# A gated long convolution and a SwiGLU FFN on one core: block order, a radix-4 transform for block 1, residuals by accumulating DMA, and a last tile in halves

## The chip, the cores and the metric

One Trainium2 chip, one core of it. The metric is device time in microseconds (us): the median of the runs of a kernel, smaller is better. Inputs and outputs are bf16; sums run in float32 in PSUM.

## The reference

For x = A_q (2048 tokens of 640 channels), with ln a layer norm without weights:

```python
k_shift = sum over t of pad(k)[t : t + S] * shift_k[:, 3 - t]      # 4 taps, causal
kv = k_shift * v
y  = irfft(rfft(kv, 2 S) * rfft(ssm_k, 2 S))[:S] + kv * ssm_D      # causal convolution of length 2048, per channel
h  = x + ln(x) * y
g, u = silu(ln(h) @ w_gate), ln(h) @ w_up                          # 640 -> 1728
out  = h + (g * u) @ w_down                                        # 1728 -> 640
```

## The kernel before

**Blocks.** The 2048 tokens are four blocks of 512. The convolution is done by blocks: each block's signal kv (`XH`) and each block of the filter (`C[0..3]`) are transformed once, and output block i is the inverse transform of a sum of products `prod(j, i)` over j <= i, kept in `Y[i]`. A task p12 is the product of signal block 1 that goes into output block 2. The filter's blocks are combined with their neighbours first (`kcomb`, L652).

**Transforms (L557 to L650).** A block of 512 tokens is read as 128 partitions by 4 token groups j (token 4p + j), so a transform is four matmul parts, one for each j, and butterflies on VectorE between them. Three forms stand side by side: `fulls` (L576) leaves all to TensorE, 64 matmuls of 128 x 320; `halves` (L557) takes 32 and one pair of additions; `quads` (L594) takes 16 and six additions in two stages. Block 0's signal goes by `fulls`, block 1's by `halves`, blocks 2 and 3 by `quads` (`R4X = (2,3)`, L354). The inverse has a two-part form (blocks 0 and 1) and a four-part form (`iquads`, blocks 2 and 3). In the two-part form token groups 0 and 2 read one of the sums (`OS`), groups 1 and 3 the other.

**Gate and second norm (`inverse`, L831).** For each token group j: matmuls (`iv`), an eviction on ScalarE that scales by the first norm's reciprocal deviation and adds 1 (`e`), a product with the centred x on VectorE (`g`: this is h less its mean), mean and squares on ScalarE (`m`, `s`), a small addition on VectorE (`v`), a power of -0.5 on GpSimd (`r`, L781), the normalization on VectorE (`n`, L912), and a transposing DMA from SP's queue into `hnT` (`ht`, L436).

**FFN (`ffn`, L917).** Each block's FFN runs in two halves of 256 tokens, that is token groups 0 and 1, then 2 and 3. Matmuls into `ps` (L943), silu and copy on ScalarE (L951, L956), the product on VectorE (L964). Then four down products `dn` (L1026), one for each token group, of 28 matmuls of 320 columns into two PSUM banks. `rs` (L1041) reads PSUM, adds the mean of x and the residual in `xh` on VectorE, and `out` stores 160 KB from SP's queue.

**Accumulating DMA.** `addto` (L553) issues from GpSimd's queue a DMA that adds one SBUF tile into another. The kernel uses it for seven half or whole products and for one sum of the filter's block 3.

**Order.** The work is a list of tasks (`_Graph.add`, L92) with their reads and writes. The order on each engine is written out by hand in `PLAN` (L256) as task numbers; a task waits for the tasks it depends on, and each engine works its list strictly in order. The lists also choose between ScalarE and VectorE where a task may run on both, and give each matmul group one of four PSUM units of two banks, which it shares in turn: a group's first matmul waits until the unit's former content has been read. `fills` puts dummy matmuls ahead of a named task: 7 ahead of `wb0` (L496) and 4 ahead of `kt0.1` (L533). SP's list holds loads, transposing DMAs and stores: a DMA whose data isn't ready holds up those behind it.

Of the kernel before, what the change touches and what calls it, by code (L numbers as in the profile page):

```python
# [50 lines left out]
class _Graph:  # L51
# [128 lines left out]
    def emit(self, block):  # L180
# [85 lines left out]
    "act":  # L266
# [10 lines left out]
    "dve":  # L277
# [10 lines left out]
    "pool":  # L288
        "17 15 16 121 159 122 168 216 186 177 226 335 336 355 364 389 394 373 382 404 399 507 532 541 559 566 550 571 674 699 "
        "708 726 717 "  # L290
        "",
    "sp":
        "0 4 2 3 6 7 10 8 236 13 9 11 293 12 14 229 228 230 294 231 461 227 292 161 232 170 188 179 235 234 462 233 628 357 366 "
        "291 282 288 285 460 375 384 629 453 534 543 456 450 459 627 561 552 701 620 710 719 728 617 777 623 626 780 774 783 "
        "",
    "units":
        "0101323321220010313213100231120202332120102331301320022011320202230231210230113011022111311232002332032013120133100202"
        "11223112023230123210032310310302310311023011302103021130213"
        "",
    "fills": {  # L300
        "wb0": ["zmem", 7],
        "kt0.1": ["zmem", 4],
# [4 lines left out]
def bass_sequential_preLN__ssm_conv_h3__swiglu_ffn__prompt_kernel(  # L307
# [34 lines left out]
    LO = (('k',3),)  # L342
# [7 lines left out]
    R4X = (2,3)  # L350
# [19 lines left out]
    with ExitStack() as es:  # L370
# [33 lines left out]
        nitab = sb("nitab", 150784 + 2048, [2, 2, 2, P])  # L404
# [9 lines left out]
        bns = sb("bns", 187936, [4, 2, 6], f32)  # L414
        mvs = sb("mvs", 187936 + 192, [4, 2], f32)
# [178 lines left out]
        def quads(name, src, dst, tmp, scale, rot):  # L594
            spot = {(0, 0): dst[:, 0, 0], (0, 1): dst[:, 0, 1], (2, 0): tmp[:, 0, 0], (2, 1): tmp[:, 0, 1],
                    (3, 1): dst[:, 1, 0], (1, 0): dst[:, 1, 1], (1, 1): tmp[:, 1, 0], (3, 0): tmp[:, 1, 1]}
            for j in (1, 3, 0, 2):
                for cs in range(2):
# [12 lines left out]
            flip = dst[:, 2]  # L611
            flip = bass.AP(flip.tensor, flip.offset + D, [list(flip.ap[0]), [-D, 2], [1, D]])
            tt2 = (("0", flip, dst[:, 1], tmp[:, 1], ALU.add, 2), ("1", dst[:, 3], dst[:, 1], tmp[:, 1], ALU.subtract, 2),
                   ("2", tmp[:, 1], dst[:, 0], tmp[:, 0], ALU.subtract, 2), ("3", tmp[:, 0], dst[:, 0], tmp[:, 0], ALU.add, 2),
                   ("4", dst[:, 0:2], tmp[:], dst[:, 2:4], ALU.add, 4), ("5", dst[:, 2:4], tmp[:], dst[:, 2:4], ALU.subtract, 4))
            for q, d, a, b, op, n in tt2:
                g.add("%s.%s" % (nm, q), "dve", lambda e, n_, d=d, a=a, b=b, op=op: e.tensor_tensor(out=d, in0=a, in1=b, op=op), ("sb", n * D),  # L617
                      r=[a, b], w=[d])

        def iquads(i):  # L620
            y = Y[i]

            def two(f0, c0, step):
# [5 lines left out]
                   ("4", y[:, 1:4:2], OS[:], y[:, 0:3:2], ALU.add, 4), ("5", y[:, 0:3:2], OS[:], y[:, 0:3:2], ALU.subtract, 4))  # L629
            for q, d, a, b, op, n in tt2:  # L630
                g.add("yb%d.%s" % (i, q), "dve", lambda e, n_, d=d, a=a, b=b, op=op: e.tensor_tensor(out=d, in0=a, in1=b, op=op), ("sb", n * D),
                      r=[a, b], w=[d])

# [18 lines left out]
        def kcomb(m, dst, own, prev):  # L652
            if m in KD:
                for f in range(2):
                    addto("kc%d.%d" % (m, f), dst[:, 2 * f:2 * f + 2], own[:, 2 * f:2 * f + 2])
                return
            g.add("kc%d.s" % m, "dve", lambda e, n: e.tensor_tensor(out=dst[:], in0=prev[:], in1=own[:], op=ALU.add), ("sb", 8 * D),  # L657
                  r=[own[:], prev[:]], w=[dst[:]])
# [61 lines left out]
        def prod(j, i):  # L720
# [43 lines left out]
            if i == j and i in R4Y:  # L764
                iquads(i)
            elif i == j and ("y", i) in MB:
# [46 lines left out]

        def hntile(i, j, q, hold):
            if i or i in HT0:
                tload("ht%d.%d" % (i, j), hnT[:, :, j * P:(j + 1) * P], q[:], P, D, r=[q[:]])
                return
            if j % 2 == 0:
                hold[0] = g.tile()
            pt, b = hold[0], j % 2  # L820
# [6 lines left out]
            g.add("hp%d.%d" % (i, j), "pe", tr, ("tr", 5), r=[q[:], ident], pw=[pt])  # L827
            d = hnT[:, :, j * P:(j + 1) * P]
            evac("hpe%d.%d" % (i, j), (d, d), lambda pt=pt, b=b: pt.h(b, 0, D).rearrange("p (c x) -> p c x", c=NC5), D, pt)

        def inverse(i):  # L831
            hold = [None]
            for j in range(4):
# [3 lines left out]
                src = Y[i][:] if full else Y[i][:, (1, 3, 0, 2)[j]] if i in R4Y else (OS[:], Y[i][:, 2:4])[j % 2]  # L837
# [21 lines left out]
                nm = "iv%d.%d" % (i, j)  # L859
# [55 lines left out]
                hntile(i, j, q, hold)  # L915

        def ffn(i):  # L917
# [89 lines left out]
            for j in range(4):  # L1007
# [5 lines left out]
                if j % 2:  # L1013
                    seq = [13] + seq[:-1]
                parts = [seq[:-4], seq[-4:]] if j == 0 else [seq]
                for part in parts:

                    def mm(e, n, pt=pt, j=j, part=part, seq=seq, x2=x2):
                        for fb in part:
                            for c in range(2):  # L1020
# [5 lines left out]
                                last = e.matmul(pt.f(c, W), gu[k, fb, j * P:(j + 1) * P], Wd[k, fb, c * W:(c + 1) * W], start=st, stop=sp)  # L1026
# [4 lines left out]
                    g.add("dn%d.%d%s" % (i, j, "b" if len(parts) > 1 and part is parts[1] else ""), "pe", mm,  # L1031
                          ("mm", W, 2 * len(part) - (13 in part)) + mode,
                          r=[gu[:, f, j * P:(j + 1) * P] for f in fbs] + [Wd[:, f] for f in fbs] + ([x, ident] if "id" in part else []),
                          pw=[pt])
                nm = "rs%d.%d" % (i, j)
# [13 lines left out]
                g.add("out%d.%d" % (i, j), "sp", lambda e, n, x=x, od=od: e.dma_start(od, x), ("st", 163840), r=[x], dma=True)  # L1049
# [17 lines left out]
        prod(0, 1)  # L1067
        ktrans(3)
        kfwd(3, K3r)
        kcomb(3, K2r, K3r, K2r)  # L1070
        prod(0, 3)
        prod(0, 2)
        gview = B_w_gate.rearrange("(c p) f -> p c f", p=P)
        uview = B_w_up.rearrange("(c p) f -> p c f", p=P)
# [57 lines left out]
```

## Time and profile before

| | us |
|---|---|
| median of 3 runs | 262.49 (261.42 to 262.93) |
| the profiled execution | 261.17 |
| its span, first to last instruction | 259.4 |
| TensorE matmul busy | 253.9 |
| VectorE busy | 204.9 |
| ScalarE busy | 185.8 |
| GpSimd busy | 44.6 |

In the profile's rows PE is TensorE's matmuls, PEld its weight loads, DVE VectorE, ACT ScalarE, POOL GpSimd, SP the queue that issues most DMAs. L1026 is line 1026 of the kernel before. A group's row reads: line, engine, operation, output <- inputs, sizes, count | busy us, mean ns of one | idle time of the engine just before them and what ended it. In the strips each digit is the busy share of one fortieth of the span in tenths. Matmuls overlap, so the length of one (about 0.3 us) is longer than its step to the next. The granted TensorE clock was 1.00 over the span.

### The profile page before, as it was taken

The numbers are of one execution on the slowest core, as the hardware profiler recorded it, in microseconds if no ns is written. First come the engines' busy times: TensorE is split into PE (matmuls) and PEld (weight loads), VectorE is DVE, ScalarE is ACT, GpSimd is POOL, SyncE is SP. The second block draws the span as 40 slices with busy tenths as digits, with TensorE's granted clock in tenths as the row PEclk, the third lists the DMA queues.
The fourth block names the chain that finished last, engine by engine and source line by source line (L and its number), as shares of the span: only waits on it lengthen the run. The fifth ranks groups of instructions, "written<-read, shape, count | busy, mean of one in ns | idle before, by whom it ended". The sixth has DMA issues, their size and how long they took to land.

```text
span 259.4 us, 5381 instructions
## 1 busy us (share of the span) xinstructions
PE 253.9 (98%) x2308; PEld 199.8 (77%) x2308; DVE 204.9 (79%) x249; ACT 185.8 (72%) x311; POOL 44.6 (17%) x37
## 2 busy tenths in 40 slices
PE   7999999999999999999999999999999999999995
PEld 2787786688888866778888766888886678888663
DVE  2899999999999999998999989999996732110323
ACT  2799999997965777977776979896976445653400
POOL 0000031625402013426030141041001101000000
PEclk9999999999999999999999999999999999999999
DMA  6999997170299500198638006389000110200022
GB/s 192 378 259 316 386 240 248 30 136 4 56 330 203 107 0 3 32 221 196 162 57 149 0 0 75 95 188 153 3 0 0 31 48 20 60 3 0 3 76 76
DMA packets 34117, 29.41 MB, mean 113 GB/s; under 512 B 20899, under 2 KB 30510, under 8 KB 34094
## 3 DMA queue, kind: packets, MB, share of 16 engines
q1 hardware_dynamic: 31648, 23.82, 33.4%
q0 software_dynamic: 2432, 5.24, 11.7%
q8 instruction: 18, 0.29, 0.5%
q14 instruction: 5, 0.04, 0.0%
q10 hardware_dynamic: 14, 0.01, 0.0%
HBM read 16.55 MB, written 2.62 MB: 74 GB/s over the span
## 4 chain that ended last, share of the span: by engine, by line
PE 44%; DVE 41%; POOL 6%; DMA 5%; issue 1%; SPq 1%; DVEq 0%
PE ps L943 23%; PE ps L1026 13%; DVE tt L725 13%; DVE Y L725 6%; POOL mv L781 5%; PE ps L585 3%; DVE C L657 3%; DVE xh L1041 3%; DMA Y<-tt 2%; DMA tab<-cst_tab 2%; DVE gu L964 2%; PE ps L567 2%; DVE US L725 2%; DVE kvo L690 2%; POOL st L781 1%; DVE XH L617 1%
## 5 line engine op out<-in xcount | busy, mean ns | idle before, releaser
L1026 PE MATMUL ps<-Wd,gu 128*128 128x320 bf16 (+1 forms) x448 | 62.2, 300 | 0.1
L1026 PEld LDWEIGHTS ps<-Wd,gu 128*128 128x128 bf16 (+1 forms) x448 | 41.1, 98 | 19.9 <-issue 3.9
L725 DVE TENSOR_TENSOR tt<-XH,C 128x2560 bf16<-128x2560 bf16 (+1 forms) x31 | 48.1, 1569 | 0.3 <-DMA Y<-tt 0.2
L964 DVE TENSOR_TENSOR gu<-gu,ub 128x1024 bf16<-128x1024 bf16 (+1 forms) x32 | 19.8, 619 | 23.7 <-ACT gu L951 17.2
L951 ACT ACTIVATE gu<-ps 128x1024 bf16<-128x1024 f32 (+1 forms) x32 | 29.1, 914 | 12.4 <-PE ps L943 12.4
L781 POOL TENSOR_TENSOR mv<-mv,half 128x1 f32<-128x1 f32 x16 | 24.6, 1539 | 58.9 <-DVE mv L779 58.9
L956 ACT ACTIVATE ub<-ps 128x1024 bf16<-128x1024 f32 x24 | 24.5, 1020 | 14.0 <-DVE gu L964 9.9
L943 PE MATMUL ps<-hnT,GB 128*128 128x256 bf16 x280 | 34.0, 273 | 0.0
L943 PE MATMUL ps<-hnT,UB 128*128 128x256 bf16 x280 | 34.0, 273 | 0.0
L943 PEld LDWEIGHTS ps<-hnT,GB 128*128 128x128 bf16 x280 | 27.3, 98 | 3.3
L943 PEld LDWEIGHTS ps<-hnT,UB 128*128 128x128 bf16 x280 | 27.3, 98 | 3.3
L943 PE MATMUL ps<-hnT,UA 128*128 128x256 bf16 x240 | 28.8, 273 | 0.2 <-ACT ub L956 0.2
L943 PE MATMUL ps<-hnT,GA 128*128 128x256 bf16 x240 | 28.6, 273 | 0.0
L784 ACT ACTIVATE qo<-xh 128x640 bf16<-128x640 bf16 x32 | 23.9, 748 | 3.1 <-DVE xh L872 1.9
L943 PEld LDWEIGHTS ps<-hnT,UA 128*128 128x128 bf16 x240 | 23.4, 98 | 3.5 <-ACT ub L956 0.5
L943 PEld LDWEIGHTS ps<-hnT,GA 128*128 128x128 bf16 x240 | 23.5, 98 | 2.9
L1041 DVE SCALAR_TENSOR_TENSOR xh<-ps,st,xh 128x640 bf16<-128x640 f32 x16 | 14.0, 879 | 13.8 <-PE ps L1026 13.8
L781 POOL TENSOR_TENSOR st<-st,half 128x4 f32<-128x4 f32 x4 | 9.4, 2351 | 80.4 <-DVE st L779 80.4
L865 ACT ACTIVATE qo<-ps,one,st 128x640 bf16<-128x640 f32 x16 | 14.0, 899 | 9.2 <-PE ps L850 7.2
L567 PE MATMUL ps<-KT,tab 128*128 128x320 bf16 x96 | 14.3, 299 | 0.2 <-DMA tab<-cst_tab 0.2
L441 ACT ACTIVATE XH<-ps 128x640 bf16<-128x640 f32 x18 | 12.4, 713 | 1.9 <-PE ps L603 1.7
L786 ACT ACTIVATE qo<-xh,mv 128x640 bf16<-128x640 bf16 x16 | 13.5, 848 | 0.1
(106 smaller groups left out, 378.2 us busy)
## 6 DMA issues: line engine op xcount, KB each, us to landing
kc<-in_A_ssm_k_dram SPq DMA_DIRECT2D x4, 640.0 KB, 7.5
xh<-in_A_q_dram SPq DMA_DIRECT2D x4, 640.0 KB, 5.9
out_dram<-xh SPq DMA_DIRECT2D x16, 160.0 KB, 1.9
C<-US POOLq DMA_DIRECT2D x4, 640.0 KB, 7.2
kvo<-in_A_v_dram SPq DMA_DIRECT2D x3, 640.0 KB, 6.0
Wd<-in_B_w_down_dram SPq DMA_DIRECT2D x1, 1280.0 KB, 10.1
Y<-US POOLq DMA_DIRECT2D x2, 640.0 KB, 6.2
GB<-in_B_w_gate_dram SPq DMA_DIRECT2D x1, 1120.0 KB, 9.6
```

Source lines behind the costliest of these rows:

```text
L567: last = e.matmul(pt.f(c, W), tab[:, f, cs, j], src[:, j, c * W:(c + 1) * W], start=(j == js[0]), stop=(j == js[1]))
L725: g.add(nm, "dve", lambda e, n_: e.tensor_tensor(out=d, in0=a, in1=b, op=op), ("sb", n * D), r=[a, b], w=[d])
L781: g.add(name + "r", "pool", lambda e, n: e.tensor_tensor(out=dst, in0=tmp, in1=hf, op=ALU.pow), ("pp", 4), r=[tmp, half[:]], w=[dst])
L784: g.add(name + "m", "act", lambda e, n: e.activation(out=junk, in_=x, func=ACTF.Identity, scale=-1.0 / D, accum_out=sm), ("aa", D, 0), r=[ ...
L786: g.add(name + "s", "act", lambda e, n: e.activation(out=junk, in_=x, func=ACTF.Square, bias=sm, accum_out=sq), ("aa", D, 1), r=[x, sm], w ...
L865: g.add(nm + "e", "act", lambda e, n, pt=pt, q2=q2, s=s, j=j: e.activation(out=q2, in_=pt.f2(W), func=ACTF.Identity, scale=s[:, 3, j:j + 1 ...
L943: last = e.matmul(pt.f(q // 2, 256, o=256 * (q % 2)), w[:, c, f0:f0 + P], hnT[:, c, cols], start=(c == 0), stop=(c == NC5 - 1))
L951: g.add("sg%d.%d%d" % (i, h, gp), "act", lambda e, n, pa=pa, gv=gv, nf=nf: e.activation(out=gv, in_=pa.f(0, 256 * nf).rearrange("p (f x) - ...
L956: g.add("su%d.%d%d" % (i, h, gp), "act", lambda e, n, pb=pb: e.activation(out=ub[:].rearrange("p b x -> p (b x)"), in_=pb.f(0, 1024), func ...
L964: g.add("mu%d.%d%d" % (i, h, gp), "dve", lambda e, n, gv=gv, ubv=ubv: e.tensor_tensor(out=gv, in0=gv, in1=ubv, op=ALU.mult), ("sb", 256 * ...
L1026: last = e.matmul(pt.f(c, W), gu[k, fb, j * P:(j + 1) * P], Wd[k, fb, c * W:(c + 1) * W], start=st, stop=sp)
L1041: g.add(nm, "dve", lambda e, n, pt=pt, x2=x2, pm=pm: e.scalar_tensor_tensor(out=x2, in0=pt.f2(W), scalar=pm, in1=x2, op0=ALU.add, op1=ALU. ...
```

## The change

The settings, and what each does:

```diff
-    LO = (('k',3),)
+    LO = (('k',3),('x',3))
+    RD = (0,1,2)
+    KS = (1,)
+    TS = ((3,3),)
+    JP = (0,1)
+    SEQ = "P01 K W F0 S1 P11 I1 P02 P12 P03 P13 F1 S2 P22 I2 P23 F2 S3 P33 I3 F3"
-    R4X = (2,3)
+    R4X = (1,2,3)
```

- `R4X`: block 1's signal is transformed by `quads`.
- `LO`: in block 3's `quads` the last sum is formed by an accumulating DMA (the two summands change places, so that it can be added in place).
- `RD`: for blocks 0 to 2 the residual is added by DMA:

```diff
+                elif i in RD:
+                    r2 = RB[:].rearrange("p (b x) -> p b x", b=2)
+                    g.add(nm, "act dve", lambda e, n, pt=pt, r2=r2, pm=pm: e.activation(
+                        out=r2, in_=pt.f2(W), func=ACTF.Identity, bias=pm) if n == "act" else e.tensor_scalar(
+                        out=r2, in0=pt.f2(W), scalar1=pm, scalar2=None, op0=ALU.add), ("rse", D), r=[pm], w=[RB[:]], pr=[pt])
+                    addto("ra%d.%d" % (i, pos(i, j)), x, RB[:])
```

- `KS`: the combination of filter block 1 is two instructions of half the size.
- `TS`: the last down product of block 3 is made in two column halves, each with its own 14 matmuls, residual and store of 80 KB:

```diff
+        def split(i, j, pt, seq):
+            x, pm = xh[i % 2][:, j, :], st1[i % 2][:, 4, j:j + 1]
+            for c in range(2):
+                def mm(e, n, c=c):
+                    for fb in seq:
+                        k = slice(0, P) if fb < 13 else slice(FL * c, FL * c + FL)
+                        last = e.matmul(pt.f(c, W), gu[k, fb, col(i, j)], Wd[k, fb, c * W:(c + 1) * W], start=fb == seq[0], stop=fb == seq[-1])
+                    return last
...
+                g.add("rs%d.%d%s" % (i, j, "ac"[c]), "dve", lambda e, n, c=c, xc=xc: e.scalar_tensor_tensor(
+                    out=xc, in0=pt.f(c, W), scalar=pm, in1=xc, op0=ALU.add, op1=ALU.add), ("stt", W), r=[xc, pm], w=[xc], pr=[pt])
```

- `JP`: in blocks 0 and 1 the inverse makes token groups 0, 2, 1, 3 in this order, and they take the columns of `hnT` in this order, so that groups 0 and 2 are the first half of the FFN:

```diff
+        def pos(i, j):
+            return (0, 2, 1, 3)[j] if i in JP else j
```

- `SEQ`: the order in which the steps are entered as tasks (P product, K block 3 of the filter, W loads of the weights, S signal, I inverse, F FFN). Before, p03 and p02 were entered ahead of block 1's signal, and p12 and p13 behind block 1's inverse.

`RB` is a new buffer of 1280 bytes; two small tables move to other addresses. The lists in `PLAN` are all written anew. By the tasks' names, where they differ most:

```
PE before:  wb0 wb4 kt0.1 kt0.0 k0t (8 of 12) kf0.011 kf0.010 kf0.111 kf0.000 .. k0t4 .. tp0.0 tp0.4 tp0.2 kf0.110 ..
PE after:   wb4 wb0 k0t (12) tp0.4 kt0.0 kt0.1 tp0.0 tp0.2 kf0.000 kf0.001 kf0.010 kf0.011 kf0.111 ..
PE before:  .. tp2.0 fu0.12 fg0.13 dn0.0 dn0.0b dn0.1 iv1.0 iv1.2 iv1.1 iv1.3 ..
PE after:   .. dn0.0 fu0.11 iv1.1 dn0.0b iv1.0 fg0.13 fu0.12 dn0.1 iv1.2 iv1.3 dn0.2 dn0.3 tp2.4 tp2.2 tp2.0 fu1.00 ..
PE after:   .. dn1.1 iv2.1 iv2.0 dn1.2 iv2.2 iv2.3 dn1.3 xf3 (8) fu2.00 ..
PE after:   .. dn2.0 dn2.0b iv3.0 iv3.1 dn2.3 iv3.2 iv3.3 dn2.2 dn2.1 fu3.00 .. dn3.1 dn3.0b dn3.3a dn3.2 dn3.3c
DVE before: .. p01 .. p03.b p03.a p02.a p03.c p02.c p03.d p02.b p02.d xb1.0 xb1.1 p11 yb1.0 ..
DVE after:  .. p01 .. xb1 (6) p11 kc3.s p02.a yb1.0 p02.c p02.b p02.d yb1.1 iv1.0g p12 p03 p13 ..
DVE after:  .. p23.0a iv2.1g yb2.5 iv2.0g kv3.4 iv2.1v rs1.2 kv3.2 iv2.0v iv2.1n kv3.0 iv2.2g iv2.0n ..
POOL after: .. ra0.0 p02.e iv1.0r ra0.1 iv1.1r ra0.2 p12.0e ra0.3 p12.1e iv1.3r iv1.2r .. ra1.0 la2r ra1.1 iv2.1r ra1.2 iv2.0r ra1.3 ..
SP before:  ident kc0 k00 k02 tab0 tab1 x0 v0 WdD kc2 ntab kc1 kT1 itab kc3 GB UA UB v1 ..
SP after:   ident k00 k02 kc0 v0 tab0 x0 tab1 kc1 ntab kc3 itab kc2 kT1 UA v1 GA PKu UB ..
```

Here kt, kf and kc are a filter block's transposes, transform and load, k0t the transposes of block 0's keys, tp a signal block's taps, xf and xb its transform and additions, yb the additions ahead of an inverse, fu and fg the FFN's two products, ra the new accumulating DMA of a residual. `fills` becomes 7 dummy matmuls ahead of `wb4` and 1 ahead of `kt0.0`; their operand is set by GpSimd in place of VectorE. Evictions also change engine: the three key tiles and both tiles of filter block 0 are evicted by ScalarE. The residual copies run on ScalarE for rs0.0 to rs0.3, rs1.0, rs1.1 and rs2.1 and on VectorE for rs1.2, rs1.3, rs2.0, rs2.2 and rs2.3.

More of the change, by code (lines that the diff above doesn't have):

```diff
@@ L655, in kcomb @@
                     addto("kc%d.%d" % (m, f), dst[:, 2 * f:2 * f + 2], own[:, 2 * f:2 * f + 2])
+                return
+            if m in KS:
+                for f in (0, 2):
+                    g.add("kc%d.s%d" % (m, f), "dve", lambda e, n, f=f: e.tensor_tensor(out=dst[:, f:f + 2], in0=prev[:, f:f + 2], in1=own[:, f:f + 2], op=ALU.add),
+                          ("sb", 4 * D), r=[own[:, f:f + 2], prev[:, f:f + 2]], w=[dst[:, f:f + 2]])
                 return
@@ L765, in prod @@
                 iquads(i)
+            elif i == j and ("y", i) in LO:
+                g.add("yb%d.0" % i, "dve", lambda e, n: e.tensor_tensor(out=OS[:], in0=y[:, 0:2], in1=y[:, 2:4], op=ALU.subtract), ("sb", 4 * D),
+                      r=[y[:]], w=[OS[:]])
+                addto("yb%d.1" % i, y[:, 2:4], y[:, 0:2])
             elif i == j and ("y", i) in MB:
@@ L1006, in ffn @@
                           e.tensor_copy(out=b, in_=a), ("cp", 256 if i in HALF else N), r=[a], w=[b])
-            for j in range(4):
+            for j in (0, 2, 1, 3) if i in JP else range(4):
                 pt = g.tile()
@@ L1012, in ffn @@
                 seq = (["id"] if onpe else []) + list(range(14))
-                if j % 2:
+                if col(i, j).start // P % 2:
                     seq = [13] + seq[:-1]
                 parts = [seq[:-4], seq[-4:]] if j == 0 else [seq]
+                if (i, j) in TS:
+                    split(i, j, pt, seq)
+                    continue
                 for part in parts:
@@ L1025, in mm @@
                                 k = slice(0, P) if fb < 13 else slice(FL * c, FL * c + FL)
-                                last = e.matmul(pt.f(c, W), gu[k, fb, j * P:(j + 1) * P], Wd[k, fb, c * W:(c + 1) * W], start=st, stop=sp)
+                                last = e.matmul(pt.f(c, W), gu[k, fb, col(i, j)], Wd[k, fb, c * W:(c + 1) * W], start=st, stop=sp)
                         return last
@@ L1030, in ffn @@
                     mode = (int(part[0] == 13), int(part[-1] == 13))
-                    g.add("dn%d.%d%s" % (i, j, "b" if len(parts) > 1 and part is parts[1] else ""), "pe", mm,
+                    g.add("dn%d.%d%s" % (i, pos(i, j), "b" if len(parts) > 1 and part is parts[1] else ""), "pe", mm,
                           ("mm", W, 2 * len(part) - (13 in part)) + mode,
-                          r=[gu[:, f, j * P:(j + 1) * P] for f in fbs] + [Wd[:, f] for f in fbs] + ([x, ident] if "id" in part else []),
+                          r=[gu[:, f, col(i, j)] for f in fbs] + [Wd[:, f] for f in fbs] + ([x, ident] if "id" in part else []),
                           pw=[pt])
-                nm = "rs%d.%d" % (i, j)
+                nm = "rs%d.%d" % (i, pos(i, j))
                 pm = st1[i % 2][:, 4, j:j + 1]
@@ L1095, in bass_sequential_preLN__ssm_conv_h3__swiglu_ffn__prompt_kernel, with filter3 @@
                 pmean(i)
-            prod(i, i)
-            inverse(i)
-            for k in range(i + 1, NB):
-                prod(i, k)
-            ffn(i)
+        def filter3():
+            ktrans(3)
+            kfwd(3, K3r)
+            kcomb(3, K2r, K3r, K2r)
+        steps = {"K": filter3, "W": weights, "S": signal, "P": prod, "I": inverse, "F": ffn}
+        for step in SEQ.split():
+            steps[step[0]](*[int(c) for c in step[1:]])
         g.arrange(PLAN)
```

108 lines of the change are left out of this document (60 added, 48 removed), and 50 rows, old and new, of the table PLAN.

## The prediction

> **What bounds the kernel now.** I read the page's first two parts, then the waits of PE alone, then the chain of work in order of time (its columns: start, length, what), then single groups. PE is TensorE's matmul row, DVE VectorE, ACT ScalarE, POOL GpSimd.
>
> ```profile
> span 259.4 us, 5381 instructions
> PE 253.9 (98%) x2308; PEld 199.8 (77%) x2308; DVE 204.9 (79%) x249; ACT 185.8 (72%) x311; POOL 44.6 (17%) x37
> ...
> PE   7999999999999999999999999999999999999995
> ...
> DVE  2899999999999999998999989999996732110323
> ...
> PEclk9999999999999999999999999999999999999999
> ```
>
> PE is full in every slice but the first and the last; DVE is nearly as full over three quarters of the span and idle after. A busy PE could still be a stretched one, so I ask what it waited for and how fast it ran.
>
> ```profile
> PE ps L488 <- DVE gu L483: 1.4, 1, 1.4
> PE ps L603 <- DVE xh L1041: 0.3, 1, 0.3
> PE ps L943 <- ACT ub L956: 0.2, 1, 0.2
> PE ps L567 <- DMA tab<-cst_tab: 0.2, 1, 0.2
> ```
>
> ```profile
> 9.10 2.33 PE ps L567 x16
> ...
> 12.20 2.40 PE ps L679 x66
> ...
> 96.22 1.45 DVE OS L547
> ...
> 159.32 3.77 PE ps L1026 x28
> ...
> 211.57 29.48 PE ps L943 x270
> 241.05 15.11 PE ps L1026 x112
> 256.16 0.03 issue
> 256.18 0.89 DVE xh L1041
> ```
>
> Those four waits, 2.1 us, are all that this view puts down. The rates are even: 28 matmuls of 320 columns in 3.77 us are 0.135 us each, 270 of 256 columns in 29.48 us are 0.109 us each. So from 9.1 us to 256.2 us PE is one queue of work. The time falls only if that queue gets shorter, or the first 9.1 or the last 3.2 us shrink, and it rises by every wait that the new order brings. The profiled run took 261.17 us, 1.8 us more than its span; the median is 262.49 us, 1.3 us above that run. I sum on the span and move the median by the same difference.
>
> **The change, part by part.** *Block 1's signal in four.* Its forward transform goes from 32 matmuls (`halves`) to 16 (`quads`).
>
> ```profile
> L567 PE MATMUL ps<-kvo,tab 128*128 128x320 bf16 x32 | 5.2, 299 | 0.0
> ...
> L617 DVE TENSOR_TENSOR XH<-OS,XH 128x2560 bf16<-128x2560 bf16 x4 | 5.9, 1485 | 0.0
> ...
> L617 DVE TENSOR_TENSOR XH<-XH,OS 128x1280 bf16<-128x1280 bf16 x4 | 3.2, 818 | 0.0
> ```
>
> 16 x 0.135 = **2.2 us** leave PE's queue. DVE pays: two additions of 1.48 us become four of 0.82 and two of 1.48, 3.3 us more. In block 3 one addition of 1.48 becomes an accumulating DMA. Splitting the sum of the second filter in two halves costs DVE about nothing (2 x 1.48 for 2.81, less the overlap of neighbours).
>
> *The residual.* For blocks 0 to 2, the 12 instructions of L1041 become a copy from PSUM that adds the mean (7 on ACT, 5 on DVE by the new lists) and an accumulating DMA on POOL's queue.
>
> ```profile
> L1041 DVE SCALAR_TENSOR_TENSOR xh<-ps,st,xh 128x640 bf16<-128x640 f32 x16 | 14.0, 879 | 13.8 <-PE ps L1026 13.8
> L865 ACT ACTIVATE qo<-ps,one,st 128x640 bf16<-128x640 f32 x16 | 14.0, 899 | 9.2 <-PE ps L850 7.2 <-DVE st L806 1.3 <-PE ps L855 0.6
> ...
> L912 DVE TENSOR_SCALAR qo<-xh,mv 128x640 bf16<-128x640 bf16 x16 | 7.0, 441 | 2.1 <-POOL mv L781 2.0
> ...
> L444 DVE TENSOR_SCALAR C<-ps 128x640 bf16<-128x640 f32 x3 | 2.5, 817 | 0.4 <-PE ps L567 0.4
> ```
>
> Seven leave DVE (0.88 each) for ACT (0.90, by L865's shape), five stay at 0.82. With some early evictions that the lists also hand to ACT, DVE's total falls by 5 us and ACT's rises by 6. Neither is the queue that ends last, so this is worth nothing by itself; its stores wait for the DMA, and all but block 3's have 45 us and more of FFN 3 behind them. If ACT's slack were gone, PSUM would come free late: up to 0.9 us per tile.
>
> *Order around block 1.* Its product now runs ahead of p02 and p03, its inverse ahead of most of FFN 0's down products. In the old order PE met DVE just there (PE row of the timeline, weight load's wait, and DVE's first product):
>
> ```profile
> 97.73 2.35 PE L855 MATMUL ps<-OS,itab 128*128 128x320 bf16 x16
> ```
> ```profile
> PEld ps L855 <- DVE OS L547: 0.4, 1, 0.4
> ```
> ```profile
> 22.10:97.70 75.60, 75.28 (x728) 59.20 (x726) 74.29 (x70) 65.32 (x108) 17.79 (x9) 1.00 0.60 167
> ```
> ```profile
> L964 DVE TENSOR_TENSOR gu<-gu,ub 128x1024 bf16<-128x1024 bf16 x24 | 16.4, 685 | 19.4 <-ACT gu L951 14.5 <-ACT ub L956 4.9
> ...
> L725 DVE TENSOR_TENSOR Y<-XH,C 128x5120 bf16<-128x5120 bf16 x2 | 5.6, 2815 | 0.0
> ```
>
> The third row has PE, weight loads, DVE, ACT and POOL from 22.1 us, where block 0's product begins on DVE, to 97.7: DVE worked 74.3 of 75.6 us. So both sides must move alike. DVE's instructions overlap by 0.08 us, so each counts by its step to the next. Out of that stretch go p03 (2 x 2.73 + 2 x 1.40 = 8.3), three instructions of p02 (4.2), three multiplications of FFN 0 (1.8) and four small ones (1.9); in come the quads (2.9) and 0.4. Block 1's sum, ready at 97.7 before (96.22 + 1.45), is ready 12.8 us sooner, with 0.1 for the start at 85.0. PE: the taps of block 2 (2.4), two FFN 0 groups (35 x 0.109 = 3.8), 36 down matmuls (4.9) and the 2.2 go out, with the start's 0.1: 97.7 - 13.2 = 84.5. PE waits **0.5 us** more; bounds 0 and 2 (DVE idles as much again as in the old stretch, and a little). FFN 0's first group comes 3.5 us sooner (the third filter's 32 matmuls, 4.4, go behind it, 0.8 of block 1's come ahead), and its first two token groups need only one of the inverse's two sums; **0.2** for it, between the same bounds' near end and nothing. The rest of p02 and p03 has until block 2, where DVE comes out 1.3 us earlier and PE 1.0. Block 3's accumulating DMA has 8 us of DVE work until its first reader.
>
> *POOL's queue.* A norm's power is now queued behind the residual's DMA issue. Issues and powers of one element, and the transposing DMA, by their own views:
>
> ```profile
> L554 POOL DMA_DIRECT2D C<-US x4: 1205/1213/1684, 132.5 to 175.8; - x4
> ```
> ```profile
> L781 POOL TENSOR_TENSOR mv<-mv,half x16: 547/898/4068, 44.5 to 217.0; 128x1 f32<-128x1 f32 x16
> ```
> ```profile
> hnT<-qo SPq DMA_TRANSPOSE x16, 2.7
> ```
>
> The tightest place is block 2. Its copy for tile 2 (`rs1.2`) stands on DVE ahead of a norm, and waits for `dn1.2`; behind it on DVE are kv3.2, iv2.0v, iv2.0n, and for those FFN 2 waits. From dn1.2's end PE has two small inverses (1.1), one down product (3.8) and eight small transforms (2.2) before FFN 2: 7.1 us. The chain is 0.82 + the issue 1.21 (kv3.2, of L964's shape, and iv2.0v beside it) + a power of 0.55 to 4.07 + 0.44 (L912) + 2.7 = 5.7 to 9.2 us, 6.1 at the median power: a wait of 0 to 2.1, and none below, since the old order shows none to save. I take **0.2**, near the median.
>
> [...]
>
> *Start.* The new SP list loads block 0's keys ahead of the filter and v ahead of the tables; the taps come ahead of the filter's transform; three of the four dummy matmuls at 5.8 us go (cover for a wait, worth nothing).
>
> ```profile
> 1.13 0.50 SPq L433 DMA_DIRECT2D kc<-in_A_ssm_k_dram  x1
> 1.68 1.07 SPq L433 DMA_DIRECT2D k0n<-in_A_k_dram  x2
> 2.79 1.11 SPq L433 DMA_DIRECT2D tab<-cst_tab  x2
> ...
> 4.49 0.50 SPq L433 DMA_DIRECT2D v<-in_A_v_dram  x1
> ```
> ```profile
> v<-in_A_v_dram SPq DMA_DIRECT2D x1, 640.0 KB, 8.6
> ...
> tab<-cst_tab SPq DMA_DIRECT2D x2, 256.0 KB, 6.2
> ```
>
> v landed at 13.1, the last of 3.15 MB; in the new list the second table is last of the same bytes, so 13.1, and the first about 10.4. The transform starts when ACT has evicted three key tiles and a filter tile and the last taps are done, which I put at 11.8 us. The old order started it at 9.1 with 2.6 us of taps and transposes still to do: 11.7. The second table is needed at 13.9. So **0.1 us** late; bounds -0.5 (loads sooner) and +2 (first table with the second).
>
> *Tail.* The last tile's two halves end one after the other: half of L1041's 0.89 us, and a store of half the size, leave the end. I estimate 0.4 + 0.2 = **0.6 us** (bounds 0.3 and 1.0; the last 3.2 us are 0.9 of DVE and 2.3 of store).
>
> **Sum:** -2.2 - 0.6 + 0.5 + 0.2 + 0.2 + 0.1 = **-1.8 us**: span 257.6, that run 259.4, median **260.7**.
>
> **The rivals.** *The queue is shorter but DVE doesn't follow* (0.18). ACT's copies now stand between its norms, and DVE waits for those. If DVE loses 1.8 us more than before on the way to block 1 or block 2, the gain is eaten: about 262.5, no change. For it: both margins are under 1 us. Against: DVE has 5 us less to do in all.
>
> *POOL's queue becomes the bound* (0.12, slower). Twelve residual issues now stand between the powers. If an issue lasts as long as the longest power, 4.07 us, and the power behind it too, block 2's chain is 0.82 + 8.14 + 0.44 + 2.7 = 12.1 us against 7.1 of cover: PE loses 5.0 in place of 0.2, the sum is +3.0, the median 265.5. It decides once issue and power together pass 3.1 us, and turns the sign at 5.1. Against: four issues of four times the bytes took 1.2 to 1.7 us beside a full DVE.
>
> *The start falls back to half speed* (0.04). The dummy matmuls took 0.43 us each at 1.5 us and 0.21 at 5.8:
>
> ```profile
> 1.45 3.17 PE L488 MATMUL ps<-gu 128*128 128x512 bf16 x7 [1.45 <-DVE gu L483]
> ...
> 5.78 1.04 PE L488 MATMUL ps<-gu 128*128 128x512 bf16 x4
> ```
>
> With fewer of them PE is, by the start worked out above, some 2.5 us busy of the 4 from 5.8 to 9.8 us. If the slow rate came back for as long as it lasted at first, 3.2 us, half of that would be lost: 1.6 us, median 262.3. [...]
>
> *The forecast* (0.66): 258.6 to 261.9.
>
> **How the numbers follow.** Half a per cent, 1.3 us, is what a measurement of this kernel can tell from no change. Of the forecast's 0.66, 0.60 lies under 261.2: faster 0.60. Its rest and the DVE and start rivals are the same: 0.28. Slower is POOL's 0.12. The range goes from 258.3 (start and tail at their good ends, 0.9 us, and the runs' own spread of 1.5) up to 263.7 (the DVE rival with the start's bad end), and leaves out POOL's rival and the forecast's lowest tenth.
>
> **What would show it.** Right: 16 fewer matmuls with PE's busy time down by 2.2 to 2.5 us, first transform near 11.8, block 1's inverse near 85 with a wait under 1 us, FFN 2's first group without a wait on the transposed tiles, and one half-size DVE instruction after the last matmul. Wrong: PE idle over 1 us at L855, L943 or L567; POOL issues over 2 us; or a DVE idle time that has grown by what it shed.

## The result, and the profile after

| | before | after |
|---|---|---|
| median of 12 runs, us | 262.45 (261.02 to 262.93) | 264.04 (260.98 to 265.00) |
| ratio, 95% interval | | 1.0065 (1.0035 to 1.0094) |
| the profiled execution, us | 261.17 | 263.87 |

The changed kernel is 0.65% slower where 0.7% faster was forecast. Runs more than 1.5% above the fastest of their kernel (one of 265.0 us here, one of 925.6 of a_lp1_fill later) count in the medians and are left out of every ratio, so a ratio can differ from that of two medians. The page of the kernel after answers to the lines shown of before (lines of the code have moved down: L943 is L991, L781 is L805, L865 is L896):

```profile
span 261.8 us, 5372 instructions
PE 253.5 (97%) x2289; PEld 199.4 (76%) x2289; DVE 199.8 (76%) x245; ACT 190.4 (73%) x318; POOL 58.8 (22%) x52
...
PE   8999999999999969999999999999999999999995
...
DVE  1399999999999959999999998999998403211242
```

DVE's total fell by 5 us as worked out, ACT's rose by 5 where 6 was forecast. PE lost 19 matmuls (16 of block 1's signal, three dummies) and only 0.4 us of busy time, because in this execution it ran at half rate for longer at the start (its 20 transposes at 5.6 us took 2.31 us; before, 20 at 6.65 us took 1.28) and because the split last tile costs more (both below). It has a hole in its 15th slice, where DVE has one too. The waits of PE in the kernel after name it:

```profile
PE ps L991 <- ACT qo L896: 2.5, 1, 2.5
PE ps L495 <- POOL half L483: 1.3, 1, 1.3
PE ps L991 <- ACT C L448: 0.6, 1, 0.6
PE ps L991 <- ACT XT L448: 0.5, 1, 0.5
PE ps L612 <- DVE RB L1094: 0.3, 1, 0.3
PE ps L699 <- ACT kT L448: 0.3, 1, 0.3
```

These are 5.5 us against 2.1 before. The timeline of the kernel after around the longest (start, length, engine, what, idle time before it):

```profile
86.90 0.16 DVE L803 TENSOR_SCALAR st<-st 128x4 f32<-128x4 f32 x1
86.98 0.68 DVE L1012 TENSOR_TENSOR gu<-gu,ub 128x1024 bf16<-128x1024 bf16 x1
87.15 5.62 POOL L805 TENSOR_TENSOR st<-st,half 128x4 f32<-128x4 f32 x1
87.58 1.48 DVE L745 TENSOR_TENSOR Y<-XH,C 128x2560 bf16<-128x2560 bf16 x1
...
90.38 1.48 DVE L554 TENSOR_TENSOR Y<-Y 128x2560 bf16<-128x2560 bf16 x1
...
92.86 0.89 ACT L896 ACTIVATE qo<-ps,one,st 128x640 bf16<-128x640 f32 x1 [3.51 <-POOL st L805]
...
93.78 0.49 DVE L903 TENSOR_TENSOR xh<-xh,qo 128x640 bf16<-128x640 bf16 x1 [1.92 <-ACT qo L896]
...
93.80 2.36 PE L991 MATMUL ps<-hnT,UB 128*128 128x256 bf16 x20 [2.46 <-ACT qo L896]
```

Read it upwards from the last row. PE waits for a PSUM unit that ScalarE empties (iv1.0e); ScalarE waits for the power of block 1's *first* norm (la1r, four columns) on GpSimd; the power starts at 87.15, and ends 0.9 us after VectorE has run dry at 91.86. In the kernel before the same instruction took 2.25 us, at 96.32, and no row of PE waited for it.

The spans differ by 2.4 us: +3.4 of waits; -2.2 for 16 matmuls; +0.3 for the split last tile on PE and -0.55 behind it (below); and +1.2 at the start, which differs from execution to execution of one and the same start (the first filter transform starts at 13.0 us here; in the profile of a_lp1, whose start is the same, at 11.8, as forecast). That is +2.2.

### The profile page after: what moved, and what is told of

Same layout as the page of the kernel before. It is cut to its first block, busy times and chain, and to the rows that moved or that the text cites. A ratio compares the mean times of both kernels' runs of the same rounds, so it can differ in the third digit from the quotient of the medians.

```text
span 261.8 us, 5372 instructions
## 1 busy us (share of the span) xinstructions
PE 253.5 (97%) x2289; PEld 199.4 (76%) x2289; DVE 199.8 (76%) x245; ACT 190.4 (73%) x318; POOL 58.8 (22%) x52
## 4 chain that ended last, share of the span: by engine, by line
PE 67%; ACT 18%; DVE 7%; POOL 5%; issue 1%; DVEq 0%; ACTq 0%; POOLq 0%
PE ps L991 40%; PE ps L1077 15%; DVE tt L745 3%; ACT C L448 3%; ACT qo L810 3%; ACT qo L808 2%; POOL st L805 2%; PE ps L699 2%; ACT qo L896 2%; PE ps L574 2%; PE ps L612 2%; ACT KT L448 2%; ACT XH L448 2%; ACT KO L448 2%; PE ps L954 2%; PE ps L495 1%
## 5 line engine op out<-in xcount | busy, mean ns | idle before, releaser
L1077 PE MATMUL ps<-Wd,gu 128*128 128x320 bf16 (+1 forms) x420 | 59.1, 300 | 0.0
L1077 PEld LDWEIGHTS ps<-Wd,gu 128*128 128x128 bf16 (+1 forms) x420 | 38.9, 97 | 18.3 <-issue 3.3
L999 ACT ACTIVATE gu<-ps 128x1024 bf16<-128x1024 f32 (+1 forms) x32 | 29.1, 916 | 12.1 <-PE ps L991 11.9
L991 PE MATMUL ps<-hnT,UB 128*128 128x256 bf16 x280 | 34.2, 273 | 2.5 <-ACT qo L896 2.5
L1004 ACT ACTIVATE ub<-ps 128x1024 bf16<-128x1024 f32 x24 | 24.5, 1023 | 14.3 <-PE ps L991 10.8
L991 PE MATMUL ps<-hnT,GB 128*128 128x256 bf16 x280 | 34.0, 273 | 0.0
L991 PEld LDWEIGHTS ps<-hnT,UB 128*128 128x128 bf16 x280 | 27.3, 98 | 6.0 <-ACT qo L896 2.7
L991 PEld LDWEIGHTS ps<-hnT,GB 128*128 128x128 bf16 x280 | 27.4, 98 | 3.4
L991 PE MATMUL ps<-hnT,UA 128*128 128x256 bf16 x240 | 28.7, 273 | 0.6 <-ACT C L448 0.6
L991 PE MATMUL ps<-hnT,GA 128*128 128x256 bf16 x240 | 28.3, 273 | 0.5 <-ACT XT L448 0.5
L991 PEld LDWEIGHTS ps<-hnT,UA 128*128 128x128 bf16 x240 | 23.3, 98 | 4.1 <-ACT C L448 0.9
L805 POOL TENSOR_TENSOR mv<-mv,half 128x1 f32<-128x1 f32 x16 | 16.8, 1055 | 42.4 <-DVE mv L803 42.3
L991 PEld LDWEIGHTS ps<-hnT,GA 128*128 128x128 bf16 x240 | 23.3, 98 | 3.7 <-ACT XT L448 0.8
L805 POOL TENSOR_TENSOR st<-st,half 128x4 f32<-128x4 f32 x4 | 15.4, 3842 | 20.9 <-DVE st L803 20.9
L561 POOL DMA_DIRECT2D xh<-RB x12 | 10.7, 893 | 37.5 <-ACT RB L1093 18.9
L896 ACT ACTIVATE qo<-ps,one,st 128x640 bf16<-128x640 f32 x16 | 14.5, 929 | 4.9 <-POOL st L805 3.5
L810 ACT ACTIVATE qo<-xh,st 128x640 bf16<-128x640 bf16 x16 | 13.3, 830 | 0.1
```

Source lines behind the costliest of these rows:

```text
L805: g.add(name + "r", "pool", lambda e, n: e.tensor_tensor(out=dst, in0=tmp, in1=hf, op=ALU.pow), ("pp", 4), r=[tmp, half[:]], w=[dst])
L810: g.add(name + "s", "act", lambda e, n: e.activation(out=junk, in_=x, func=ACTF.Square, bias=sm, accum_out=sq), ("aa", D, 1), r=[x, sm], w ...
L896: g.add(nm + "e", "act", lambda e, n, pt=pt, q2=q2, s=s, j=j: e.activation(out=q2, in_=pt.f2(W), func=ACTF.Identity, scale=s[:, 3, j:j + 1 ...
L991: last = e.matmul(pt.f(q // 2, 256, o=256 * (q % 2)), w[:, c, f0:f0 + P], hnT[:, c, cols], start=(c == 0), stop=(c == NC5 - 1))
L999: g.add("sg%d.%d%d" % (i, h, gp), "act", lambda e, n, pa=pa, gv=gv, nf=nf: e.activation(out=gv, in_=pa.f(0, 256 * nf).rearrange("p (f x) - ...
L1004: g.add("su%d.%d%d" % (i, h, gp), "act", lambda e, n, pb=pb: e.activation(out=ub[:].rearrange("p b x -> p (b x)"), in_=pb.f(0, 1024), func ...
```

## The experiments

18 kernels ran, each with 6 to 12 runs beside runs of the kernel before on the same chip (medians 262.4 to 262.9). "After" stands for the changed kernel, 264.04. Edits of the lists are shown by the tasks' names.

**1. The order on GpSimd's queue (a_lp1), and the dummy matmuls (a_fill, a_lp1_fill).** In the kernel after, the mean lp1 (3.1 us, also beside DVE) stands ahead of the power la1r on GpSimd's list; a_lp1 exchanges the two. a_fill puts four dummies back, and a_lp1_fill does both.

```diff
 pool: .. kb3.1
-lp1 la1r
+la1r lp1
 ra0.0 ..
```
```diff
     "fills": {
         "wb4": ["zmem", 7],
+        "k0t0.0": ["zmem", 4],
         "kt0.0": ["zmem", 1],
```

> The kernel after, with one pair on GpSimd's list exchanged: block 1's norm power (la1r) ahead of its mean (lp1). Theory 1 (the power stands behind the mean, both beside products on VectorE, and keeps the eviction of the inverse and with it a PSUM unit): the wait of 2.5 us of PE at L991 goes, the time falls from 264.0 to about 261.5, ratio to before 0.997. Rival (that wait only takes the place of one that comes next, on VectorE or ScalarE): the wait goes and the time stays at 263.5 to 264.5.

> The kernel after with four dummy matmuls put ahead of k0t0.0, where the kernel before has four ahead of kt0.1. Theory 2 (with fewer dummies PE stays at half its rate until 9.8 us): the first transform starts near 11.8 in place of 13.0 us, the time falls by about 1.2 us to 262.8, ratio to before 1.001. Rival (the start is set by loads and evictions, or ScalarE bounds the stretch behind it anyway): the first full-rate matmul comes earlier, but FFN 0's first group still starts near 53.2 us and the time stays at 264.

> The kernel after with both edits, the power ahead of the mean and the four dummy matmuls. If both causes are real and add: 264.0 less 2.5 less 1.2 = 260.3, ratio to before 0.992. If only the power counts: 261.5. If neither: 264.

Measured: 263.97 (ratio 1.0067, 1.0040 to 1.0093); 265.55 (1.0091, 1.0051 to 1.0130); 265.14 (1.0093, 1.0055 to 1.0130). Both theories fall. In a_lp1 the power starts as soon as its input is there and still takes 5.6 us, and the wait is still 2.5: the mean was not in its way. With the dummies the medians are 1.2 to 1.5 us higher, though the intervals overlap, and the profiles show a reason:

```profile
5.63 2.31 PE L521 MATMUL ps<-idall,k0n 128*128 128x128 bf16 x20
```
```profile
5.55 1.29 PE L519 MATMUL ps<-idall,k0n 128*128 128x128 bf16 x20
...
11.78 4.52 PE L572 MATMUL ps<-KT,tab 128*128 128x320 bf16 x32
```
```profile
5.63 1.89 PE L494 MATMUL ps<-gu 128*128 128x512 bf16 x4
7.32 2.28 PE L520 MATMUL ps<-idall,k0n 128*128 128x128 bf16 x20
...
13.92 4.52 PE L573 MATMUL ps<-KT,tab 128*128 128x320 bf16 x32
```

These are the starts of after, a_lp1 and a_fill. PE leaves its half rate either early, near 5.6 us (a_lp1: 20 transposes in 1.29 us), or late, mostly between 9 and 10.5 us (after, a_fill: 2.31 and 2.28 for the 20) and in the profile of a_g_halves only near 12, where 20 more transposes took 2.34 us at 9.6. After, a_lp1 and a_g_halves have one and the same start of the program. The four dummies didn't bring the early case in their two profiles, and a dummy that runs at half rate is only a delay (1.89 us in a_fill). The runs of the kernel before fall in two groups, perhaps for this reason: in one set 10 lie at 260.6 to 261.5 us and 15 at 262.4 to 263.2.

**2. What a wait of PE costs (a_busy).** Eleven dummies of 0.215 us ahead of an FFN group in front of the wait; nothing else moves.

```diff
     "fills": {
         "wb4": ["zmem", 7],
         "kt0.0": ["zmem", 1],
+        "fg0.13": ["tab0", 11],
```

> The kernel after with 11 dummy matmuls of 512 columns (2.4 us) put just ahead of the FFN group in front of the wait of 2.5 us, so that PE is busy in place of idle and the wait itself shrinks to under 0.5 us; no other work is moved. Theory 4 (the wait costs twice: its 2.5 us, and then about 3.5 us at half clock in most runs, 1.8 us): the clock reads 1.0 in all runs and the time falls by about 1 to 1.8 us, to 262.3 to 263. Rival (the clock has nothing to do with the wait): clock 0.993 as often as before, time 264 or more.

Measured: 263.08 (1.0023, 1.0002 to 1.0045), 1.0 us below after (the two intervals overlap a little), with no row of L991 behind ACT's qo any more and the clock at 1.0 (0.999 once) in all 12 runs; after shows 0.992 to 0.994 in 6 of 12. The granted clock by windows of 1 us, in a_lp1 (window, its length, PE busy and matmuls, clock, DMA share, GB/s):

```profile
90.00:91.00 1.00, 0.08 (x1) 1.00 0.00 0
91.00:92.00 1.00, 0.00 (x0) 1.00 0.00 0
92.00:93.00 1.00, 0.47 (x4) 0.96 0.00 0
93.00:94.00 1.00, 1.00 (x7) 0.50 0.96 147
94.00:95.00 1.00, 1.00 (x7) 0.50 0.63 95
95.00:96.00 1.00, 1.00 (x6) 0.50 1.17 189
96.00:97.00 1.00, 1.00 (x8) 0.83 1.15 175
```

Behind the wait of 2.5 us come 3.4 us at half clock: seven matmuls in a us where there should be ten, 1.7 us more. So the wait costs 2.5 us in half of the runs and, by this working, 4.2 in the others. The whole times don't show that difference: the six runs of after at 0.992 to 0.994 have a median of 264.2 us, the six others 263.9. The start, which also differs between runs, may hide it; that is not shown. Nor is it shown why only some of the runs are hit.

**3. Why the power is slow (a_g, a_win).** In a_g the first consumer on DVE moves up, so that DVE stops behind the norm; in a_win one wait is added.

```diff
 dve: .. la1v mu0.10
+iv1.0g
 p02.b p02.d yb1.1
-iv1.0g
 mu0.11 ..
```
```diff
             byname[name].deps.add(byname[fill[0]])
+        byname["p02.b"].deps.add(byname["la1r"])
```

> The kernel after with one VectorE instruction moved: the first product of block 1's second norm (iv1.0g) stands right behind the norm's variance and one FFN product, ahead of p02's last two and of yb1.1. Theory 3: GpSimd's power (la1r, 5.6 us for 1.0 of work) ends only once VectorE's two-input instructions stop; the move makes VectorE stop at once, so the power takes 1 to 2.3 us, the wait of 2.5 us of PE at L991 goes, and with it the half clock that follows the wait in most runs (0.993 of 262 us, 1.8 us). Time 264.0 to 260.0 (259.5 to 261.3), clock 1.0 in all runs, ratio to before 0.991. Rival (VectorE is the bound there: what it loses by idling comes back as a wait further on, at yb1.1 or the norms): 262.5 to 264. Second rival (the power is slow by itself): it stays over 5 us and the time is 264 or more.

> The kernel after, all orders as they are, with one wait added: p02.b on VectorE waits for block 1's norm power (la1r) on GpSimd. VectorE stops for about 1 us in place of running two-input products for 5 us beside the power, and stopped 1.9 us behind them before. Theory 3 with what the kernel a_g showed (the power took 1.4 us once VectorE stopped, but VectorE then idled 3.0 us and its lateness came back): the power takes 1.0 to 1.6 us, the eviction of the inverse comes at 88 us and the wait of 2.5 us goes, VectorE is 1 us earlier than in the kernel after from there on, nothing comes back, clock 1.0; time 264.0 to 260.3 (259.5 to 261.5), ratio to before 0.992. Rival (VectorE is the bound from 54 to 107 us and gives the wait back later, as in a_g): 262.5 to 264.

Measured: a_g 265.23 (1.0077, 1.0045 to 1.0109); a_win 264.98 over 12 runs in two groups of six, 260.9 to 264.1 and 265.8 to 268.1 (clock 1.0 and 0.987 to 0.994); the ratio of the lower group is 0.9983 (0.9948 to 1.0019). That a pause of DVE frees the power is shown: the power takes 1.4 us in the profiles of all ten kernels here that have the pause. It takes 5.6 in after and in five of the six others that leave DVE without a pause; the sixth is a_v2 (below). PE's wait of 2.5 us is gone with the pause. The time fell less than forecast. In a_g DVE idled 3.0 us, and its lateness came back at FFN 1. The timeline and PE's first wait in a_g, then the same wait and one of DVE's in a_win (both executions, of 267.3 and 267.5 us, lie well above their kernel's median; in the place of a_g's 6.1 us, a_g_halves has 2.2 and a_g_notail 4.0):

```profile
85.52 1.41 POOL L803 TENSOR_TENSOR st<-st,half 128x4 f32<-128x4 f32 x1
...
89.03 0.49 DVE L901 TENSOR_TENSOR xh<-xh,qo 128x640 bf16<-128x640 bf16 x1 [3.00 <-ACT qo L894]
```
```profile
PE ps L989 <- DMA hnT<-qo: 6.1, 1, 6.1
```
```profile
PE ps L990 <- DMA hnT<-qo: 5.2, 1, 5.2
...
DVE tt L744 <- DMA Y<-tt: 3.2, 1, 3.2
```

By what means DVE's instructions hold the power up, 5.6 us against 1.4, the traces do not show, and a_v2 (next) shows that the pause isn't the whole of it.

**4. A transfer in the way (a_v2, a_win_v2, a_win_v2k).** In a_win's profiled run, one of its upper group, the accumulating DMA of p02 (640 KB) took 10.2 us beside the load of v for block 2 (640 KB, 8.8), and DVE waited for its source. The load moves ahead of the first store on SP's list, and in a_win_v2k it also waits for the sum of filter block 3.

```diff
 sp: .. WdA
+v2
 out0.0
-v2
 ht1.0 ..
```
```diff
         byname["p02.b"].deps.add(byname["la1r"])
+        byname["v2"].deps.add(byname["kc3.s"])
```

> The kernel after with only the load of v for block 2 moved ahead of the first store. Theory 3 alone (the power beside VectorE's products is the wait): PE still waits 2.5 us at L991 and the time stays at 263 to 264. Rival (DMA traffic at 92 to 101 us is the cause): 262 or less.

> The kernel a_win with one DMA moved on SP's list: the load of v for block 2 (640 KB) ahead of the first store (out0.0) in place of behind it, so that it runs near 66 us and not at 92 to 101 us beside the accumulating DMA of p02. Theory 5 (in a_win's disturbed runs that addition took 10.2 us beside the load, VectorE waited 3.2 us for its source buffer, block 1's norms came late and PE waited 5.2 us for the transposed tiles and then ran at half clock): the addition takes 6.3 to 7 us, the waits go, all runs lie between 258.5 and 261.5, median 259.5 to 260.5, ratio to before 0.990. Rival (the addition is late by its own chain, not by the load): two groups of runs as in a_win, 261 and 266 to 268.

> The kernel a_win_v2 with the load of v for block 2 held back until the sum of the filter's block 3 (kc3.s, ends near 79 us), so that it runs alone between 79 and 86 us, behind the accumulating DMA of that sum and ahead of that of p02. Theory 6 (three transfers of 640 KB each have a place of their own; each pair that meets makes VectorE wait 1 to 3 us): no wait of VectorE for K3r or tt, PE waits under 1 us at hnT, clock 1.0 in all runs; 259.8 us where the clock comes up early and 261.5 where late, median 260.5 to 261.5, ratio to before 0.995. Rival (VectorE stays late by its own sum): 263 to 264 and PE waits 2 us at hnT.

Measured: a_v2 262.23 (1.0009, 0.9980 to 1.0038); a_win_v2 264.17 (1.0104, 1.0062 to 1.0147); a_win_v2k 261.49 (0.9968, 0.9940 to 0.9996). At 66 us the load meets the addition of filter block 3 instead, which then takes 8.7 to 9.3 us in place of 6.5, and DVE waits 1.2 to 1.8 us for it: a_win_v2 misses its expectation, and PE waits 2.1 us for the transposed tiles. a_v2, which has no pause, gains all the same, and comes near its rival's 262: in its profile DVE runs on without a gap and the power takes 1.4 us, as if it had slipped in between two of DVE's instructions. Traffic beside the power is no explanation, since the DMA share is 0.00 from 86 to 93 us in after and from 88 to 92 in a_v2. So a pause is enough, and not always needed; what decides it there stays open. In a_win_v2k the load stands between the two additions, at 78.6 us, is alone, and takes 3.8 us. Its transfers, then PE's waits:

```profile
kvo<-in_A_v_dram SPq DMA_DIRECT2D x1, 640.0 KB, 3.8
Y<-tt POOLq DMA_DIRECT2D x1, 640.0 KB, 6.9
```
```profile
PE ps L495 <- POOL half L483: 1.3, 1, 1.3
PE ps L991 <- ACT XT L448: 1.0, 1, 1.0
PE ps L991 <- ACT qo L808: 0.7, 1, 0.7
PE ps L612 <- DVE RB L1094: 0.6, 1, 0.6
PE ps L699 <- ACT kT L448: 0.3, 1, 0.3
PE ps L991 <- DMA hnT<-qo: 0.2, 1, 0.2
```

All 12 runs of a_win_v2k lie at 260.3 to 263.0, at clock 1.0 (0.999 once), so a_win's upper group is gone with the load's move. That the load held up the addition there is seen in the one profile only: beside the load the same addition took 6.4 us in a_win_halves. a_win_v2k is faster than both kernels: by 0.3% than before, which its interval only just clears, and by 1.0% than after in the medians.

**5. What the quads are worth (b_quad, and halves against quads).** b_quad is the kernel before with `R4X = (1,2,3)` alone, the additions ahead of block 1's product; the others are kernels above with `R4X` set back.

```diff
-    R4X = (1,2,3)
+    R4X = (2,3)
```

> The kernel before with one part of the change alone, block 1's signal by quads, its six additions in place of two on VectorE ahead of block 1's product. The prediction's term: 16 matmuls of 0.135 us off PE's queue, 2.2 us, 260.3 and ratio 0.992, if VectorE's 3.3 us more are hidden. Rival (VectorE, 74.3 of 75.6 us busy on the way to block 1, is late by them): PE waits 1 to 3 us at block 1's inverse (L855) and the ratio is 0.996 to 1.004.

> The kernel after with block 1's signal by halves, as before the change, and all else of the change kept. The prediction's term of the quads: 266.2, 2.2 us slower than after. Rival (VectorE ends 3.3 us earlier ahead of block 1's product, so the power meets an idle VectorE sooner and the wait of 2.5 us and its half clock go): 263 to 264.3, no slower.

> The kernel a_g with block 1's signal by halves again, 32 matmuls and two additions of 1.48 us in place of 16 and six additions. The prediction's term: 2.2 us slower than a_g. Rival (VectorE, which sheds 3.3 us of additions ahead of block 1, is the bound there): within 1 us of a_g.

> The kernel a_win with block 1's signal by halves (16 more matmuls on PE, 3.3 us less on VectorE). If PE alone bounds once the power is out of the way: 2.2 us slower than a_win. If VectorE bounds on the way to block 1 and 2: within 1 us of a_win or faster.

> The kernel a_win_v2 with block 1's signal by halves. If VectorE no longer bounds: 2.2 us slower than a_win_v2, the prediction's term. If VectorE still bounds on the way to block 1 and 2, as a_win_halves at 261.1 to 262.1 us suggests: no slower, within 0.7 us.

> The same kernel with block 1's signal by halves. If PE alone bounds: 2.2 us slower than a_win_v2k, the prediction's term. If VectorE bounds: within 0.7 us.

| kernel | with quads | with halves |
|---|---|---|
| before | 268.47 (1.0214, 1.0171 to 1.0258) | 262.5 |
| after | 264.04 (1.0065, 1.0035 to 1.0094) | 263.87 (1.0028, 0.9993 to 1.0063) |
| a_g | 265.23 | 265.06 (1.0110, 1.0072 to 1.0148) |
| a_win | 264.98 (0.9983, 0.9948 to 1.0019) | 261.73 (0.9988, 0.9958 to 1.0017) |
| a_win_v2 | 264.17 | 264.83 (1.0106, 1.0067 to 1.0146) |
| a_win_v2k | 261.49 | 261.56 (0.9979, 0.9949 to 1.0010) |

Nowhere are the quads worth 2.2 us. In the medians they are from 0.7 better to 3.3 worse, and 6 worse in the old order. The 3.3 of a_win come from its upper group, which a_win_halves has in one run of 12; by the ratios those two are equal. The waits of PE in b_quad and in a_win_v2k_halves (to be read against a_win_v2k's above):

```profile
PE ps L942 <- ACT ub L955: 4.7, 1, 4.7
```
```profile
PE ps L495 <- POOL half L483: 1.3, 1, 1.3
PE ps L991 <- ACT XT L448: 0.8, 1, 0.8
PE ps L699 <- ACT kT L448: 0.5, 1, 0.5
PE ps L612 <- DVE RB L1094: 0.3, 1, 0.3
```

In b_quad the additions put DVE, 74 of 75.6 us busy on that way, late: 4.7 us of wait, then half clock, which lasted 6.8 us, 5.8 of them under matmuls (2.9 lost), less 2.2: +5.4, measured 6.0. In a_win_v2k PE's waits take back 1.2 us of the gain; the rest of the difference isn't resolved, since these two profiles differ at the start as well (first transform 12.5 and 11.4 us).

**6. The residual by DMA (a_win_nord).** `RD = ()`, the twelve additions back on DVE, seven of them at places that I chose by the ends of their down products; no copies, no accumulating DMA for them.

> The kernel a_win with the residuals of blocks 0 to 2 added on VectorE again, 12 instructions of 0.88 us reading PSUM and xh, no copies and no accumulating DMA for them. The prediction's term (neither engine ends last, worth nothing): within 0.7 us of a_win. Rival (VectorE bounds around block 1 and 2, four of these fall there): 2 to 4 us slower.

Measured: 268.66 (1.0249, 1.0214 to 1.0283), 7 us above a_win's lower group and 3.7 above the median of all its runs. All six runs show a clock of 0.987 to 0.994, so half clock is part of the 7. Its profile has PE behind DVE where four of the twelve fall, ahead of FFN 1:

```profile
PE ps L990 <- DVE C L744: 4.8, 1, 4.8
...
PE ps L990 <- DVE xh L1097: 1.2, 1, 1.2
```

One placement was tried, so this is its price and no general one. With the additions at these places on DVE, moving them away is worth far more than nothing; whether a better placement would cost nothing is not shown.

**7. The tail (b_tail, a_g_notail).** b_tail is the kernel before with `TS = ((3,3),)` alone; a_g_notail is a_g with `TS = ()`.

> The kernel before with the last tile in halves alone, made from the code after the change with all other settings and lists as before. The prediction's term: 0.6 us faster (bounds 0.3 and 1.0), 261.9 where before shows 262.5, ratio 0.998; the last matmul ends 2.65 us ahead of the span's end in place of 3.2. Rival (the stores' fixed part decides): no change.

> The kernel a_g with the last down product whole again, one residual instruction of 0.89 us and one store of 160 KB behind it. The prediction's term: 0.6 us slower than a_g (bounds 0.3 and 1.0). Rival (the store's fixed part decides): within 0.2 us.

Measured: b_tail 262.56 (1.0005, 0.9976 to 1.0033); a_g_notail 266.22 (1.0118, 1.0072 to 1.0163), 1.0 us above a_g, but both kernels spread over 3 to 6 us, so that pair decides nothing. The chain of b_tail in order of time:

```profile
252.51 3.77 PE ps L1075 x28
256.29 2.02 PE ps L952 x14
258.31 0.03 issue
258.33 0.55 DVE xh L958
```

What follows the last matmul fell from 3.2 us to 2.7 (span 261.0), as forecast. But 14 matmuls of one column half take 2.02 us, 0.144 each against 0.135 in a whole product, so the two halves cost PE 0.25 to 0.3 us more. That leaves about 0.25 us, below what this measurement resolves.

## Why the prediction was wrong, step by step

- **What bounds the kernel**: PE's one queue, right for the kernel before. But its neighbour DVE, "74.3 of 75.6 us" busy, was noted and then treated as cover. It is the second bound on the way to blocks 1 and 2, and what is added to it or held behind it comes back on PE.
- **Block 1's signal in four, -2.2**: the matmuls left, the gain didn't stay (experiment 5). The rival that DVE doesn't follow, at 0.18, had part of this, with half of the price and another cause: it had DVE wait for ScalarE's copies, and the runs have ScalarE and DVE wait for GpSimd's power.
- **Order around block 1, +0.5 and +0.2**: here the sum failed, with one wait of 2.5 us at L943 (now L991), over the 1 us that the prediction had named as a sign of being wrong. The meeting of PE and DVE at the inverse was worked out well: the inverse started at 84.9 in a_lp1, with no wait, for a forecast of 84.5 to 85. But the step counted sums and matmuls, and not the next link: the inverse's eviction needs the first norm's power, which the new lists put behind the sum with 5 us of two-input DVE work beside it: 5.6 us in place of 2.25. The medians missed the sum by 3.4 us (+1.6 for -1.8). In the profiles PE's waits rose by 3.4, 2.5 of it this one wait, where the sum had 0.9 (0.5, 0.2 and 0.2); the rest of the miss is not divided up, since the start and the half clock differ from run to run. The spread of the powers, 0.55 to 4.07 us, was in the text, and was used for block 2 only, where there was no wait.
- **The half clock**: not in the sum. A wait was priced at its own length; by the 3.4 us at half clock behind it in a_lp1 it can cost 1.7 us more here, in half of the runs (experiment 2).
- **The residual, "worth nothing"**: not so with the one other placement that was tried (experiment 6), where DVE is later still.
- **POOL's queue, the slower rival**: the engine was right, the place and the price wrong. The issues took 0.9 us each, and block 2's chain had no wait; the bound was one power in block 1.
- **Start, +0.1**: right where the full rate comes up early (11.4 to 11.9 in seven profiles). The rival of a fall back to half speed had a wrong mechanism: no profile shows a fall back at the start, but the full rate can come up late (12.4 to 13.9 for the first transform). The start of the kernel before has both cases too: its first transform is at 9.1 us, and at 10.8 in b_tail, which starts alike.
- **Tail, -0.6**: right behind the last matmul (0.55), without PE's 0.3 for the split product.

## What to carry to other kernels

When an order is changed, follow each moved product to its eviction and list all that the eviction needs, small GpSimd instructions above all: beside a VectorE that never pauses one of these took four times as long here (5.6 us in after, 1.4 with a pause, though a_v2 had 1.4 without one), and one planned wait of 0.9 us on VectorE took away 2.5 on TensorE. A wait of TensorE like the one of 2.5 us here is to be priced with a chance of half clock behind it (3.4 us of it in the profile of a_lp1, none in that of after). And saving matmuls by additions on an engine that is 98% busy need not be a saving: 2.2 us of matmuls brought 0.7 us at most in the six pairs here.

## What the runs showed of the hardware

- With one and the same program start the full rate comes up early or late: 20 transposes at 5.6 us took 1.29 us in some profiles (a_lp1) and 2.31 in others (after), and 20 more at 9.6 us took 2.34 in a_g_halves; the granted clock reads 1.00 from 0 to 12 us in the profile of after, which has the 2.31.
- A wait of PE of 2.5 us was followed by 3.4 us at half clock in the profile of a_lp1 and by none in that of after. Waits of 4.7 to 6.1 us (b_quad, a_win_nord, a_win, a_g) came with 3.4 us of half clock once and 6.8 three times, and it set in before the wait had ended (at 85.4 us in b_quad, where PE went on at 86.4).
- A power of 128 x 4 on GpSimd: 1.0 us beside a VectorE that idled for the first 0.7 us of it (196.4 us of the kernel before), 1.4 with 0.9 us of pause, 5.6 beside four two-input instructions in a row. Yet it took 2.25 at 96.3 us in the kernel before and 1.4 in a_v2, where such instructions also ran on. In all of these but the first it ended 0.9 us after one of them had ended; which one is not explained.
- Two transfers of 640 KB at once, one of them accumulating: the load of v for block 2 took 3.8 us alone and 6.7 to 8.8 where it was issued behind the addition of p02. That addition took 6.3 to 7.4 without the load and 6.4 to 8.2 beside it, 10.2 once (a_win).
